# A first work list in another order, with idle matmuls, six strided loads a unit, and constants on another queue

## The chip, the cores and the metric

One core of a Trainium2 chip runs the whole program. The metric is the time of one execution in microseconds of the device. Three runs of the kernel before gave 1581.33, 1581.92 and 1584.39 us, median 1581.92.

## The reference

Retention attention without a softmax, and two feed-forward blocks, all in float32:

```
scores = (q @ k.T) / sqrt(64);  ret = scores * gamma_h**(row - col) for row >= col
x = (ret @ v), heads side by side           # 8 batches, 8 heads, 576 rows, 64 wide -> 4608 x 512
x = ((x @ w1) * (x @ w2)) @ w3 @ w_out      # 512 -> 1024 -> 1024 -> 512
h = x @ w_in;  out = (h - tanh(h)) @ w_out2 # 512 -> 2048 -> 512
```

The weights come in as 64-bit floats, and every product keeps float32 accuracy.

## The kernel before

A product of float32 accuracy is made of three matmuls of a rounded type (`mm3`, L121): each operand is split in a high and a low part. A weight tile (128 x 512) is converted from 64 bit by a `Conv` in steps: `load` (SP's queue), `a` (ScalarE), `b1` to `b4` (VectorE), `c` (ScalarE, the high part), `d1` (the value less its high part, L183) and `d2` (plus the rest, L186). 16 of them, `J[0]` to `J[15]`, make w1 and w2.

Attention runs over 40 chunks, five a batch, of 128 rows (the last of a batch 64). For the first ten the rows are loaded as they lie (256 KB each for q, k and v), scaled, turned on TensorE (`TQ`, `TK`, tiles psq and psk), copied by ScalarE (`CQ`, `CK`), multiplied to scores and to an update of the running state (`SC`, tile psx), masked and summed by VectorE (`PT`, `ST`), and multiplied with v and state (`VA`, tile pso). Then the result is split into its parts x (`RE`, `AD`, `HI`, `LO`). The later 30 chunks are loaded in strided blocks instead, 32 DMAs for half a batch (`load_qk`, L326), which are held in a list `pend` and issued a few at a time by `trickle(n)` (L341) on SP's queue; VectorE then turns them in 32 x 32 blocks (`stage_0`, tiles kT and qT).

The first feed-forward products are 96 units (t, m): 12 tiles of 384 rows by 8 column blocks. A unit is two halves of 12 matmuls (`half_s`, tile psab, four banks), of which ScalarE copies the first (`pf_copy`, L475) and VectorE multiplies the second on (`pf_mult`, L479); the product is stored in DRAM.

Three things set the order. Up to the end of unit 16 it is the list `plan` (L683): a string of tokens, carried out one after the other, where each appends its instructions to its engines' queues. `H0.1.0` is the first half of unit (0, 1), `F`, `G` and `P` its copy, product and store, `Z0` to `Z15` issue four strided loads each, `K`, `X`, `Y`, `V` prepare chunk 10. Behind the list a loop (L760) runs the other 80 units: each starts with up to two steps of a side job (conversions of the other weights, and their product), then the store of an earlier unit, then `trickle(TRK)`, then its two halves, then the attention stages due by a table that places a new chunk every 2.26 units. `need` (L346) issues at once whatever of a tile is still held when a stage wants it. After the units come the two products of the rest, from DRAM.

Each engine carries out its own queue in order; a DMA issued by SP or ScalarE stands in that engine's queue.

Of the kernel before, what the change touches and what calls it, by code (L numbers as in the profile page):

```python
# [8 lines left out]
F32 = mybir.dt.float32  # L9
# [11 lines left out]
P1 = 0.68482121  # L21
# [7 lines left out]
def retention_glu_tanh_kernel(  # L29
# [16 lines left out]
    PE, ACT, DVE, POOL, SP = nc.tensor, nc.scalar, nc.vector, nc.gpsimd, nc.sync  # L46

    B, H, S, D = q.shape
    NT, DM = out.shape
    P = 128  # L50
# [18 lines left out]
    psm = ctx.enter_context(tc.tile_pool(name="psm", bufs=4, space=PSUM))  # L69
# [8 lines left out]
        return slots.tile([P, 2048], F32R, tag=f"s{i}", name=name)  # L78

    cst = cpool.tile([P, 2 * P + 4], F32, name="cst")  # L80
    SP.dma_start(out=cst, in_=consts)
    ident = cst[:, 0:P]
    mask = cst[:, P:2 * P]
    b_p1 = cst[:, 2 * P:2 * P + 1]
# [1 line left out]
    b_mk = cst[:, 2 * P + 2:2 * P + 3]  # L86
    NB32 = S // W
    dec = cpool.tile([P, 2 * H * NA + NP * NB32], F32, name="dec")
    SP.dma_start(out=dec, in_=decay)
    dec_q = dec[:, 0:H * NA].rearrange("p (c h) -> p c h", h=H)  # L90
    dec_v = dec[:, H * NA:2 * H * NA].rearrange("p (c h) -> p c h", h=H)
    dec_b = dec[:, 2 * H * NA:].rearrange("p (g j) -> p g j", g=NP)
# [21 lines left out]
    def tick():  # L114
        for e in held:
            e[0] -= 1
        for _, eng, o, i_ in [e for e in held if e[0] <= 0]:
            eng.dma_start(out=o, in_=i_)
        held[:] = [e for e in held if e[0] > 0]
# [221 lines left out]
    def trickle(n):  # L341
        for _ in range(min(n, len(pend))):
            _, o, i_ = pend.pop(0)
            SP.dma_start(out=o, in_=i_)  # L344
# [152 lines left out]
    def w12_target(m, i):  # L497
        def f(j):
            if i == 0:
                ws[m] = slot(m, f"w12_{m}")  # L500
            j.high = ws[m][:, i * 1024:i * 1024 + 512]
            j.low = ws[m][:, i * 1024 + 512:i * 1024 + 1024]
        return f

    def rows(w):

        return tuple(w[o:o + DM // 2].rearrange("(k p) c -> p k c", p=D) for o in (0, DM // 2))

    J = [
        Conv(rows((w1, w2)[i][:, m * P:m * P + P]), target=w12_target(m, i), pool="head")  # L510
        for m in range(FF) for i in range(2)
    ]
# [115 lines left out]
    ACT.activation(warm, warm, AF.Copy)  # L628
    px = {}
    pu = {}  # L630

    def natural(i, k):
        attn_load(i, "qkv"[k])
# [29 lines left out]
    def four(z):  # L663
# [2 lines left out]
            load_qk(2, 1)  # L666
        trickle(4)

    act = {
        "Lq": lambda i: natural(i, 0), "Lk": lambda i: natural(i, 1), "Lv": lambda i: natural(i, 2),  # L670
        "SQ": lambda i: scale(POOL if i else DVE, A[i][0], dec_q, i),
# [4 lines left out]
        "RE": rest, "AD": add_rest, "HI": x_high, "LO": low_part,  # L676
        "LJ": lambda j: J[j].load(), "a": lambda j: J[j].a(), "c": lambda j: J[j].c(),
        "b1_": lambda j: J[j].b1(), "b2_": lambda j: J[j].b2(), "b3_": lambda j: J[j].b3(), "b4_": lambda j: J[j].b4(),
        "d1_": lambda j: J[j].d1(POOL), "d2_": lambda j: J[j].d2(),
        "H": part_ab, "F": first, "G": second, "P": stored,  # L680
        "Z": four, "K": load_kv, "X": stage_q, "Y": stage_0, "V": stage_v,
    }
    plan = """  # L683
    Lq0 Lk0 Lv0 Lq1 Lk1 Lv1 SQ0 LJ0 TQ0 Lq2 Lk2 TK0 CQ0 Lv2 SV0 CK0 Lq3 Lk3 SC0 SQ1 Lv3 LJ1 PT0 TQ1 ST0 TK1 CQ1
    LJ2 SV1 CK1 VA0 Lq4 SC1 RE0.1 Lk4 HI0.0 AD0.1 HI0.1 Lv4 LO0.0 PT1 a0 LJ3 LO0.1 ST1 SQ2 Lq5 Lk5 b1_0 VA1 b2_0
    Lv5 TQ2 RE1.0 b3_0 RE1.1 AD1.0 c0 TK2 SV2 AD1.1 b4_0 HI1.0 HI1.1 d1_0 LJ4 LO1.0 CK2 LO1.1 CQ2 SQ3 d2_0 TK3
    SC2 CK3 SV3 TQ3 PT2 CQ3 ST2 SC3 a1 b1_1 VA2 PT3 b2_1 RE2.0 RE2.1 AD2.0 c1 AD2.1 ST3 HI2.0 SQ4 HI2.1 LO2.0 a2
    VA3 b3_1 SV4 LO2.1 RE3.0 TK4 b4_1 RE3.1 H0.0.0 CK4 d1_1 LJ5 AD3.1 AD3.0 HI3.1 b1_2 HI3.0 b2_2 Lq6 Lk6 LO3.0
    c2 TQ4 d2_1 Lv6 F0.0 SQ5 LO3.1 Lq7 CQ4 H0.0.1 b3_2 a3 Lk7 b1_3 d1_2 Lv7 b4_2 Lq8 b2_3 SC4 SV5 G0.0 Lk8 TQ5
    c3 d2_2 P0.0 TK5 CQ5 PT4 H0.1.0 CK5 b3_3 a4 b1_4 d1_3 b4_3 VA4 F0.1 b2_4 Lv8 SC5 RE4.0 d2_3 c4 LJ6 AD4.0 a5  # L690
    H0.1.1 b3_4 PT5 d1_4 HI4.0 LJ7 LO4.0 ST5 SQ6 TK6 G0.1 VA5 CK6 P0.1 b4_4 SV6 LJ8 b1_5 TQ6 HI5.0 d2_4 RE5.1
    CQ6 SQ7 LO5.0 H0.2.0 AD5.1 b2_5 HI5.1 LO5.1 c5 b3_5 SC6 F0.2 SV7 b4_5 LJ9 TQ7 PT6 d1_5 TK7 CQ7 ST6 Lq9 CK7
    SQ8 Lk9 TK8 d2_5 Lv9 VA6 CK8 H0.2.1 RE6.0 RE6.1 AD6.0 SV8 AD6.1 HI6.0 HI6.1 LO6.0 LO6.1 SC7 G0.2 P0.2 a6
    b1_6 H1.2.0 PT7 b2_6 ST7 c6 H1.0.0 F1.2 b3_6 a7 b1_7 d1_6 b4_6 H1.2.1 LJ10 b2_7 F1.0 d2_6 c7 b3_7 a8 b1_8
    d1_7 H1.1.0 G1.2 P1.2 b4_7 LJ11 b2_8 H1.0.1 d2_7 c8 b3_8 a9 SQ9 b1_9 b4_8 d1_8 VA7 LJ12 G1.0 b2_9 F1.1
    H1.1.1 SV9 RE7.1 P1.0 d2_8 RE7.0 c9 AD7.0 AD7.1 HI7.0 b3_9 HI7.1 TQ8 G1.1 d1_9 a10 H0.3.0 P1.1 LO7.0 b4_9
    CQ8 LJ13 LO7.1 d2_9 SC8 F0.3 b1_10 b2_10 H1.3.0 a11 PT8 c10 b3_10 ST8 d1_10 H0.3.1 b4_10 LJ14 b1_11 d2_10
    F1.3 VA8 b2_11 a12 G0.3 c11 H1.3.1 P0.3 b3_11 RE8.1 RE8.0 b1_12 d1_11 AD8.0 AD8.1 HI8.0 b4_11 HI8.1 H0.4.0
    LJ15 LO8.0 G1.3 LO8.1 P1.3 d2_11 Z0 H1.4.0 F0.4 b2_12 a13 b1_13 c12 b3_12 Z1 b2_13 d1_12 H0.4.1 F1.4 b4_12
    c13 b3_13 d2_12 d1_13 Z2 H1.4.1 a14 G0.4 b4_13 b1_14 P0.4 d2_13 TK9 Z3 TQ9 a15 G1.4 H0.5.0 b2_14 CK9 CQ9  # L700
    b1_15 P1.4 c14 b3_14 Z4 b2_15 d1_14 SC9 F0.5 b4_14 c15 H1.5.0 PT9 Z5 d2_14 b3_15 VA9 F1.5 b4_15 d1_15 Z6
    H0.5.1 RE9.0 AD9.0 d2_15 HI9.0 LO9.0 Z7 H1.5.1 G0.5 P0.5 H0.6.0 G1.5 K10 P1.5 Z8 H1.6.0 F0.6 X10 X11 Y10 Z9
    H0.6.1 F1.6 Z10 V10 H1.6.1 G0.6 P0.6 Z11 H0.7.0 G1.6 P1.6 H1.7.0 F0.7 Z12 H0.7.1 F1.7 Z13 H1.7.1 Z14 G0.7
    P0.7 G1.7 Z15 P1.7
    """
    for tok in plan.split():
        op = max((o for o in act if tok.startswith(o)), key=len)
# [30 lines left out]
    stages.append((p + 3, cluster, (len(chunks) - 1,)))  # L738
    stages.sort(key=lambda e: e[0])

    TRK = 8
    NO = 84
    side_n = {}
    sn = 0
# [15 lines left out]
    for n, (t, m) in list(enumerate(units))[N0:]:  # L760
# [18 lines left out]
        tick()  # L779
        trickle(TRK)  # L780
        pss = []
# [48 lines left out]
    for n, (t, f) in enumerate(py):  # L830
        p_load(n + 3)
        p_split(n + 2)
        if f == 0:
            pool, tag = (psa, "a") if t % 2 == 0 else (psm, "m")
# [196 lines left out]
```

## Time and profile before

| | |
|---|---|
| median of the runs | 1581.92 us |
| profiled execution | 1582.95 us |
| its span, first to last instruction | 1581.2 us |
| TensorE busy | 1547.8 us (98%), 11312 matmuls |
| VectorE busy | 1075.4 us (68%) |
| ScalarE busy | 773.0 us (49%) |
| POOL busy | 111.3 us (7%) |

The profile is one execution. A busy TensorE is not one at its peak: matmuls overlap, and the clock that was granted to it changes, so the start of one matmul after the other tells more than the length of one. "Idle before" an instruction is the time its engine stood, with what ended the wait behind it.

### The profile page before, as it was taken

The page shows a single profiled execution, that of the slowest core. Times are in us where ns is not written, and L with a number is a line of the kernel's source. Part 1 is how long each engine was busy: PE and PEld are TensorE (multiplying, and loading weights), DVE is VectorE, ACT ScalarE, POOL GpSimd, SP SyncE. Part 2 cuts the span into 40 slices and gives each one's busy share as a digit, 9 for nine tenths or more (in the row PEclk, how much of TensorE's full clock was granted, in tenths as well). Part 3 has the DMA queues.
Part 4 walks back from the last instruction along what each step waited for, and adds up shares of the span by engine and source line. Part 5 has one row for each costly group of instructions (what it writes and reads, how often), then busy time and mean ns, then how long its engine had stood idle before and what let it go on. Part 6 is the DMA issues. An engine that isn't in the chain of part 4 may idle for free.

```text
span 1581.2 us, 28518 instructions
## 1 busy us (share of the span) xinstructions
PE 1547.8 (98%) x11312; PEld 1346.0 (85%) x11312; DVE 1075.4 (68%) x1792; ACT 773.0 (49%) x1408; POOL 111.3 (7%) x102
## 2 busy tenths in 40 slices
PE   6999999999999999999999999999999999999999
PEld 5899889999999998888888888888888888888887
DVE  4884766557543567676477777767777777778676
ACT  3431222222221233444376666676676766767665
POOL 3531211111111000000000000000000000000000
PEclk7999999999999999999999999999999999999999
DMA  9856776575756386776460101010010101010000
GB/s 192 175 124 141 172 175 148 140 175 119 158 163 162 115 263 231 249 242 221 167 246 1 47 7 41 14 40 14 0 54 1 47 7 48 7 40 8 27 1 27
DMA packets 265926, 166.45 MB, mean 105 GB/s; under 512 B 206656, under 2 KB 235840, under 8 KB 264384
## 3 DMA queue, kind: packets, MB, share of 16 engines
q1 hardware_dynamic: 264352, 155.06, 36.6%
q10 hardware_dynamic: 1440, 9.57, 1.6%
q8 instruction: 89, 1.46, 0.4%
q14 instruction: 45, 0.37, 0.1%
HBM read 114.24 MB, written 50.33 MB: 104 GB/s over the span
## 4 chain that ended last, share of the span: by engine, by line
PE 85%; DMA 4%; DVE 4%; SPq 3%; issue 2%; ACT 1%; POOL 0%; DVEq 0%; ACTq 0%
PE psh L126 8%; PE psh L124 8%; PE psout L125 8%; PE psout L126 8%; PE psh L125 8%; PE psout L124 8%; PE psab L124 5%; PE psab L125 5%; PE psab L126 5%; PE psy L126 4%; PE psy L124 4%; PE psy L125 4%; SPq L344 2%; PE pso L416 2%; DMA raw<-in_moe_w_out_dram 1%
## 5 line engine op out<-in xcount | busy, mean ns | idle before, releaser
L124 PE MATMUL psab<-x,w 128*128 128x384 f32 x768 | 263.3, 343 | 7.3 <-ACT pf L475 7.2
L125 PE MATMUL psab<-x,w 128*128 128x384 f32 x768 | 259.6, 338 | 2.3 <-DVE w L186 2.3
L126 PE MATMUL psab<-x,w 128*128 128x384 f32 x768 | 259.1, 337 | 0.0
L124 PE MATMUL psh<-yhl,w2i 128*128 128x512 f32 x576 | 225.5, 392 | 0.0
L126 PE MATMUL psh<-yhl,w2i 128*128 128x512 f32 x576 | 225.3, 391 | 0.0
L125 PE MATMUL psout<-w2o,g 128*128 128x512 f32 x576 | 224.5, 390 | 0.0
L126 PE MATMUL psout<-w2o,g 128*128 128x512 f32 x576 | 224.3, 389 | 0.0
L124 PE MATMUL psout<-w2o,g 128*128 128x512 f32 x576 | 224.2, 389 | 0.0
L125 PE MATMUL psh<-yhl,w2i 128*128 128x512 f32 x576 | 224.0, 389 | 0.0
L920 ACT ACTIVATE g<-w 128x512 fp32r<-128x512 f32 x144 | 90.4, 628 | 168.1 <-DVE w L915 168.1
L908 DVE TENSOR_TENSOR w<-u,psh 128x512 f32<-128x512 f32 x144 | 97.8, 679 | 105.8 <-ACT th L902 105.8
L124 PEld LDWEIGHTS psab<-x,w 128*128 128x128 f32 x768 | 145.9, 190 | 11.0 <-ACT pf L475 8.4
L125 PEld LDWEIGHTS psab<-x,w 128*128 128x128 f32 x768 | 146.0, 190 | 3.4 <-DVE w L186 3.1
L126 PEld LDWEIGHTS psab<-x,w 128*128 128x128 f32 x768 | 146.0, 190 | 0.0
L921 DVE TENSOR_TENSOR g<-w,g 128x512 fp32r<-128x512 f32 x144 | 99.5, 691 | 50.4 <-ACT g L920 50.4
L433 ACT ACTIVATE rest<-pso 128x128 f32<-128x128 f32 x64 | 15.1, 275 | 232.6 <-PE pso L416 232.6
L126 PEld LDWEIGHTS psh<-yhl,w2i 128*128 128x128 f32 x576 | 108.1, 188 | 24.1
L125 PEld LDWEIGHTS psh<-yhl,w2i 128*128 128x128 f32 x576 | 108.2, 188 | 23.6
L124 PEld LDWEIGHTS psout<-w2o,g 128*128 128x128 f32 x576 | 108.1, 188 | 22.9
L125 PEld LDWEIGHTS psout<-w2o,g 128*128 128x128 f32 x576 | 108.1, 188 | 22.6
L126 PEld LDWEIGHTS psout<-w2o,g 128*128 128x128 f32 x576 | 108.1, 188 | 22.6
L124 PEld LDWEIGHTS psh<-yhl,w2i 128*128 128x128 f32 x576 | 108.1, 188 | 22.6
(91 smaller groups left out, 2666.4 us busy)
## 6 DMA issues: line engine op xcount, KB each, us to landing
pdr<-pf SPq DMA_DIRECT2D x96, 192.0 KB, 3.9
pin<-pdr SPq DMA_DIRECT2D x36, 512.0 KB, 4.5
raw<-in_moe_w_out_dram SPq DMA_DIRECT2D x24, 512.0 KB, 4.4
ydr<-ys ACTq DMA_DIRECT2D x9, 1024.0 KB, 4.3
out_dram<-os SPq DMA_DIRECT2D x35, 256.0 KB, 2.2
kn<-in_k_dram SPq DMA_DIRECT2D x32, 256.0 KB, 4.2
vn<-in_v_dram SPq DMA_DIRECT2D x32, 256.0 KB, 4.5
raw<-in_moe_w_dram SPq DMA_DIRECT2D x32, 256.0 KB, 5.7
```

The costliest lines, as they stand in the source:

```text
L124: PE.matmul(ps, lh, rh, start=first, stop=False)
L125: PE.matmul(ps, ll, rh, start=False, stop=False)
L126: PE.matmul(ps, lh, rl, start=False, stop=last)
L344: SP.dma_start(out=o, in_=i_)
L416: PE.matmul(po[y][D * hf:D * hf + D, o * D:o * D + D], lhs, rhs, start=not any(x[:2] == (y, hf) for x in mm[:k]), stop=not any(x[:2] == (y ...
L433: ACT.activation(w, A[i][1 - s][:, KD * D:KD * D + NP // 2 * D].rearrange("p (k q) -> p k q", q=D), AF.Copy)
L908: DVE.tensor_tensor(w, u, h, op=ALU.mult)
L920: ACT.activation(g[:, 0, :], w, AF.Copy)
L921: DVE.tensor_tensor(g[:, 1, :], w, g[:, 0, :].bitcast(F32), op=ALU.subtract)
```

## The change

Four edits. The list is another one: the same tokens in another order, and new tokens `D`, each of which puts so many matmuls of the 128 x 128 identity by itself into TensorE's queue (45 in all); their result is read by nobody. `d1` of the 16 conversions in the list moves from POOL to VectorE. The two constant loads are issued by ScalarE and no longer by SP. `TRK`, the strided loads that each unit behind the list issues, is 6 and no longer 8.

```diff
-    SP.dma_start(out=cst, in_=consts)
+    ACT.dma_start(out=cst, in_=consts)
...
-    SP.dma_start(out=dec, in_=decay)
+    ACT.dma_start(out=dec, in_=decay)
...
+    wps = []
...
+    def warm_up(k):
+        if not wps:
+            wps.append(psm.tile([P, 512], F32, tag="m", name="pswarm"))
+        for _ in range(k):
+            PE.matmul(wps[0][:, :P], ident, ident, start=True, stop=True)
...
-        "d1_": lambda j: J[j].d1(POOL), "d2_": lambda j: J[j].d2(),
+        "d1_": lambda j: J[j].d1(DVE), "d2_": lambda j: J[j].d2(),
...
-        "Z": four, "K": load_kv, "X": stage_q, "Y": stage_0, "V": stage_v,
+        "Z": four, "K": load_kv, "D": warm_up, "X": stage_q, "Y": stage_0, "V": stage_v,
...
-    Lq0 Lk0 Lv0 Lq1 Lk1 Lv1 SQ0 LJ0 TQ0 Lq2 Lk2 TK0 CQ0 Lv2 SV0 CK0 Lq3 Lk3 SC0 SQ1 Lv3 LJ1 PT0 TQ1 ST0 TK1 CQ1
+    Lq0 Lk0 Lv0 LJ0 Lq1 SQ0 Lk1 Lv1 D8 TQ0 Lq2 TK0 CQ0 Lk2 CK0 Lv2 SV0 LJ1 D5 SC0 Lq3 Lk3 PT0 a0 Lv3 b1_0 ST0
...
-    TRK = 8
+    TRK = 6
```

TensorE, from its first matmul on, before: psq and psk are the turned q and k of a chunk, psx its scores and updates, pso its outputs.

```order
L262 MATMUL psq<-cst,qn 128x128 x4
L262 MATMUL psk<-cst,kn 128x128 x4
L297 MATMUL psx<-qT,kT 64x64 x16
L278 MATMUL psx<-vn,kn 64x64 x16
L262 MATMUL psq<-cst,qn 128x128 x4
L262 MATMUL psk<-cst,kn 128x128 x4
L416 MATMUL pso<-pt,vn 64x64 x16
L416 MATMUL pso<-qT,state_127 64x64 x8
```

The same place now, pswarm being the tile of the idle matmuls:

```order
L674 MATMUL pswarm<-cst 128x128 x8
L262 MATMUL psq<-cst,qn 128x128 x4
L262 MATMUL psk<-cst,kn 128x128 x4
L674 MATMUL pswarm<-cst 128x128 x5
L297 MATMUL psx<-qT,kT 64x64 x16
L278 MATMUL psx<-vn,kn 64x64 x16
L674 MATMUL pswarm<-cst 128x128 x7
L416 MATMUL pso<-pt,vn 64x64 x16
L416 MATMUL pso<-qT,state_127 64x64 x8
L262 MATMUL psq<-cst,qn 128x128 x4
L262 MATMUL psk<-cst,kn 128x128 x4
```

Idle matmuls stand ahead of the first transposes, of the scores and of the outputs, and the outputs of chunk 0 go ahead of the transposes of chunk 1.

VectorE in the first conversion, before, from the masks of chunk 0 on (pt masked scores, ct and cf the conversion's tiles, x the parts of the attention's result):

```order
L307 TENSOR_TENSOR pt<-psx,mask_129 128x4x64 x2
L287 COPY state_127<-psx 128x256
L289 TENSOR_TENSOR state_128<-psx,state_127 128x256
L440 TENSOR_TENSOR pso<-pso,rest 128x2x64
L447 TENSOR_TENSOR x<-pso,x 128x4x64
```

And now:

```order
L307 TENSOR_TENSOR pt<-psx,mask_129 128x4x64 x2
L153 TENSOR_SCALAR ct<-raw 128x512
L287 COPY state_127<-psx 128x256
L289 TENSOR_TENSOR state_128<-psx,state_127 128x256
L157 SCALAR_TENSOR_TENSOR cf<-cf,ct 128x512
L162 TENSOR_SCALAR ct<-cf 128x512
L447 TENSOR_TENSOR x<-pso,x 128x4x64
L440 TENSOR_TENSOR pso<-pso,rest 128x2x64
L165 SCALAR_TENSOR_TENSOR ct<-raw,ct 128x512
L447 TENSOR_TENSOR x<-pso,x 128x4x64
L183 TENSOR_TENSOR cf<-cf,w_0_298 128x512
```

The conversion begins between the first masks and the first states, and its d1 (L183) is an instruction of this queue; before, POOL had the 16 of them between its scalings.

SP behind the list, before (raw are weight tiles of the side job, kn and vn of a later chunk, qb_1925 and kb_1926 the strided blocks of batch 3's first half, pdr the stores):

```order
L145 DMA raw<-in_moe_w_out_dram 128x512 x2
L360 DMA kn<-in_k_dram 128x8x64
L360 DMA vn<-in_v_dram 128x8x64
L344 DMA qb_1925<-in_q_dram 32x8x32 x8
L118 DMA pdr_69<-pf 128x384
L344 DMA qb_1925<-in_q_dram 32x8x32 x8
L360 DMA kn<-in_k_dram 128x8x64
L360 DMA vn<-in_v_dram 128x8x64
L145 DMA raw<-in_moe_w_out_dram 128x512
L118 DMA pdr_69<-pf 128x384
L344 DMA kb_1926<-in_k_dram 32x8x32 x8
```

And now, the same blocks as qb_1971 and kb_1972:

```order
L145 DMA raw<-in_moe_w_out_dram 128x512 x2
L360 DMA kn<-in_k_dram 128x8x64
L360 DMA vn<-in_v_dram 128x8x64
L344 DMA qb_1971<-in_q_dram 32x8x32 x6
L118 DMA pdr_69<-pf 128x384
L344 DMA qb_1971<-in_q_dram 32x8x32 x6
L360 DMA kn<-in_k_dram 128x8x64
L360 DMA vn<-in_v_dram 128x8x64
L145 DMA raw<-in_moe_w_out_dram 128x512
L118 DMA pdr_69<-pf 128x384
L344 DMA qb_1971<-in_q_dram 32x8x32 x4
L344 DMA kb_1972<-in_k_dram 32x8x32 x2
```

A weight load of the side job has fewer strided issues ahead of it, and the keys of the half batch go out later.

## Rows read from the trace of the kernel before

**Rows 1.** Windows by stage: length, busy PE PEld DVE ACT POOL, clock, DMA, GB/s.

```profile
0.00:37.00 37.00, 22.90 (x532) 19.74 (x532) 16.90 (x37) 12.18 (x28) 14.64 (x19) 0.79 1.07 190
37.00:81.10 44.10, 41.45 (x596) 37.82 (x596) 38.14 (x70) 19.66 (x44) 22.24 (x16) 0.95 0.80 171
81.10:129.30 48.20, 47.39 (x427) 45.66 (x426) 32.22 (x62) 16.10 (x34) 15.43 (x11) 1.00 0.59 133
129.30:215.00 85.70, 76.74 (x1026) 73.14 (x1026) 59.31 (x117) 21.19 (x51) 13.80 (x12) 0.94 0.72 161
215.00:594.00 379.00, 376.06 (x4417) 358.78 (x4416) 211.53 (x435) 86.45 (x207) 45.17 (x45) 1.00 0.62 161
594.00:1581.20 987.20, 983.29 (x4322) 810.85 (x4320) 717.32 (x1074) 617.38 (x1047) 0.00 (x0) 1.00 0.21 72
```

**Rows 2.** Windows of core 0 with half the granted clock, same columns.

```profile
28.20:38.30 10.10, 6.91 (x162) 6.19 (x155) 6.78 (x15) 3.45 (x11) 4.54 (x4) 0.50 1.15 194
...
154.50:157.70 3.20, 3.20 (x12) 3.20 (x11) 1.07 (x4) 0.66 (x2) 0.00 (x0) 0.50 0.95 189
202.30:208.90 6.60, 4.89 (x40) 4.46 (x44) 2.15 (x4) 1.55 (x3) 0.97 (x1) 0.50 0.97 221
```

**Rows 3.** Chain of waits, 0 to 70 us: start us, us, what.

```profile
5.97 1.11 PE psq L262 x4
...
59.17 0.62 PE psx L297 x32
59.80 0.47 PE psx L278 x32
60.26 0.58 PE psq L262 x4
...
62.11 1.09 PE pso L416 x64
...
63.58 0.17 PE psab L125
```

**Rows 4.** Tile psab, 37 to 129.3 us: count, ns min/median/max, first, last start.

```profile
L124 PE MATMUL psab<-x,w x128: 334/334/687, 37.0 to 128.8; 128*128 128x384 f32 x128
```

**Rows 5.** Timeline of SP, first issues: start us, us, what.

```profile
0.74 0.39 SPq L81 DMA_DIRECT2D cst<-in_consts_dram  x1
...
1.65 0.43 SPq L250 DMA_DIRECT2D qn<-in_q_dram  x1
```

**Rows 6.** Timeline of VectorE, 0 to 40 us: start us, us, what, [idle before].

```profile
22.74 1.52 DVE L186 TENSOR_TENSOR w<-cf,ct 128x512 fp32r<-128x512 f32 x1 [0.50 <-POOL cf L183]
...
38.88 0.68 DVE L186 TENSOR_TENSOR w<-cf,ct 128x512 fp32r<-128x512 f32 x1
```

**Rows 7.** VectorE by line, 0 to 129.3 us: count, busy us, mean ns, idle.

```profile
L447 DVE TENSOR_TENSOR x<-pso,x 128x256 fp32r<-128x256 f32 x18 | 7.3, 413 | 0.3 <-ACT x L443 0.3
```

**Rows 8.** POOL by line, 0 to 129.3 us, same columns.

```profile
L183 POOL TENSOR_TENSOR cf<-cf,w 128x512 f32<-128x512 f32 x16 | 25.0, 1565 | 43.1 <-DVE ct L162 24.4 <-ACT w L180 5.3 <-ACT pf L475 4.0
```

**Rows 9.** Timeline of POOL, 20 to 24 us.

```profile
22.67 1.04 POOL L256 TENSOR_TENSOR qn<-qn,dec 128x512 f32<-128x512 f32 x1
```

**Rows 10.** Timeline of SP's queue, strided loads and a weight load.

```profile
106.20 7.87 SPq L344 DMA_DIRECT2D kb<-in_k_dram  x16
...
193.03 4.94 SPq L344 DMA_DIRECT2D kb<-in_k_dram  x8
198.08 0.40 SPq L145 DMA_DIRECT2D raw<-in_moe_w_out_dram  x1
...
199.00 4.22 SPq L344 DMA_DIRECT2D kb<-in_k_dram  x8
```

**Rows 11.** Timeline of ScalarE, 200 to 204 us.

```profile
202.40 0.66 ACT L149 ACTIVATE cf<-raw 128x512 f32<-128x512 f32 x1 [6.07 <-DMA raw<-in_moe_w_out_dram]
```

**Rows 12.** Waits of TensorE, 129.3 to 215 us: us in total, times, longest.

```profile
PE psab L124 <- ACT pf L475: 6.5, 2, 3.9
```

**Rows 13.** Timeline of VectorE, 212 to 217 us.

```profile
214.92 0.70 DVE L387 STREAM_TRANSPOSE kT<-kb 128x512 f32<-128x512 f32 x1
```

More of the change, by code (lines that the diff above doesn't have):

```diff
@@ L685, in retention_glu_tanh_kernel @@
[L685 to L704, printed above, removed]
+    Lq0 Lk0 Lv0 LJ0 Lq1 SQ0 Lk1 Lv1 D8 TQ0 Lq2 TK0 CQ0 Lk2 CK0 Lv2 SV0 LJ1 D5 SC0 Lq3 Lk3 PT0 a0 Lv3 b1_0 ST0
@@ new lines, in retention_glu_tanh_kernel @@
+    Lq4 SQ1 Lk4 D7 VA0 b2_0 Lv4 TQ1 HI0.0 b3_0 RE0.1 LJ2 TK1 LO0.0 c0 SV1 AD0.1 CQ1 LJ3 HI0.1 b4_0 CK1 LO0.1 SQ2
+    LJ4 D6 SC1 d1_0 Lq5 TK2 PT1 SV2 Lk5 TQ2 CK2 ST1 CQ2 d2_0 D2 SC2 VA1 a1 b1_1 PT2 Lv5 RE1.0 b2_1 RE1.1 AD1.0
+    SQ3 c1 AD1.1 ST2 HI1.1 HI1.0 D8 TQ3 b3_1 LO1.0 SV3 TK3 CQ3 LO1.1 VA2 CK3 b4_1 LJ5 d1_1 SC3 RE2.0 RE2.1 AD2.0
+    SQ4 AD2.1 HI2.0 Lq6 PT3 HI2.1 Lk6 SV4 LO2.0 Lv6 ST3 a2 LO2.1 D9 VA3 d2_1 b1_2 H0.0.0 RE3.1 b2_2 RE3.0 a3
+    AD3.1 AD3.0 HI3.1 b3_2 HI3.0 b1_3 TQ4 c2 LO3.0 H0.0.1 F0.0 b4_2 CQ4 LJ6 LO3.1 d1_2 b2_3 Lq7 TK4 CK4 Lk7 SQ5
@@ new lines, in retention_glu_tanh_kernel @@
+    G0.0 TK5 c3 b3_3 P0.0 SC4 Lv7 CK5 d2_2 TQ5 PT4 SV5 a4 H0.1.0 CQ5 b1_4 d1_3 b4_3 VA4 F0.1 LJ7 b2_4 SC5 RE4.0
+    d2_3 c4 AD4.0 SQ6 a5 H0.1.1 b3_4 PT5 HI4.0 LO4.0 d1_4 TQ6 SV6 G0.1 TK6 CQ6 P0.1 ST5 CK6 b4_4 VA5 LJ8 b1_5
+    SC6 d2_4 RE5.1 HI5.0 AD5.1 a6 SQ7 LO5.0 H0.2.0 HI5.1 PT6 LO5.1 b2_5 TQ7 F0.2 ST6 c5 TK7 b3_5 CQ7 SV7 VA6
+    b1_6 CK7 b4_5 RE6.1 SC7 RE6.0 LJ9 d1_5 AD6.0 d2_5 HI6.0 Lq8 LO6.0 a7 H0.2.1 Lk8 AD6.1 Lv8 b2_6 HI6.1 LO6.1
+    c6 b3_6 H1.1.0 G0.2 P0.2 d1_6 b4_6 LJ10 PT7 H1.0.0 F1.1 d2_6 ST7 a8 H1.2.0 F1.0 SQ8 b1_7 b1_8 b2_7 b2_8 c7
@@ new lines, in retention_glu_tanh_kernel @@
+    H1.1.1 b3_7 SV8 c8 b3_8 F1.2 d1_7 VA7 G1.1 P1.1 b4_7 H1.0.1 RE7.1 RE7.0 LJ11 AD7.1 AD7.0 HI7.1 d2_7 HI7.0
+    LO7.0 a9 TK8 G1.0 TQ8 P1.0 LO7.1 CK8 b4_8 H1.2.1 CQ8 LJ12 d1_8 b1_9 d2_8 Lq9 SC8 Lk9 a10 G1.2 b2_9 P1.2
+    H0.3.0 Lv9 PT8 c9 Z0 b3_9 ST8 H1.3.0 F0.3 d1_9 Z1 b4_9 SQ9 b1_10 H0.3.1 F1.3 LJ13 d2_9 b2_10 a11 Z2 H1.3.1
+    SV9 G0.3 c10 b3_10 b1_11 b4_10 P0.3 H0.4.0 Z3 G1.3 d1_10 b2_11 H1.4.0 P1.3 d2_10 F0.4 LJ14 c11 b3_11 a12
+    b1_12 Z4 d1_11 H0.4.1 b4_11 b2_12 F1.4 LJ15 d2_11 c12 H1.4.1 G0.4 a13 Z5 b3_12 b1_13 d1_12 VA8 G1.4 P0.4
@@ L705, in retention_glu_tanh_kernel @@
+    b4_12 P1.4 H0.5.0 RE8.0 Z6 RE8.1 AD8.0 AD8.1 HI8.0 d2_12 HI8.1 LO8.0 a14 H1.5.0 b2_13 Z7 F0.5 LO8.1 c13
+    b3_13 b1_14 H0.5.1 b4_13 K10 d1_13 Z8 b2_14 H1.5.1 d2_13 c14 G0.5 a15 b3_14 P0.5 F1.5 b1_15 Z9 H0.6.0 d1_14
+    G1.5 b4_14 P1.5 b2_15 Z10 H1.6.0 F0.6 d2_14 c15 b3_15 X10 Z11 TQ9 d1_15 TK9 CQ9 H0.6.1 CK9 b4_15 X11 Y10 Z12
+    V10 SC9 G0.6 H1.6.1 PT9 P0.6 Z13 F1.6 d2_15 VA9 G1.6 Z14 H0.7.0 RE9.0 AD9.0 HI9.0 LO9.0 P1.6 H1.7.0 F0.7 Z15
+    H0.7.1 F1.7 H1.7.1 G0.7 P0.7 G1.7 P1.7
     """
```

## The prediction

> **What bounds the kernel now.** I read the stages first [rows 1]: six stretches of the span, with each engine's busy time, the granted clock and the transfer rate. The reader is to see that TensorE sits idle 14.1 us of the first 37.0, 2.7 of the next 44.1, 0.8 of the next 48.2, 9.0 of the 85.7 after that, 2.9 of the 379 up to 594 us and 3.9 of the last 987. So all that can be won lies before 215 us, and what is won there is kept, because nothing later waits for anything but TensorE. The same rows show two other limits: in the first 37 us the transfers are at 1.07 of the engines' time and 190 GB/s, and from 37 to 81 us VectorE is busy 38.1 of 44.1 us.
>
> The second view is the clock [rows 2]. From 28 to 38 us, in a stretch at 154 us and in one at 202 us the granted clock is 0.50, that is 1.2 GHz, each time behind a wait of TensorE. The price is seen in the chain of waits [rows 3]: four 128-column transposes take 1.11 us at the start and 0.58 us later.
>
> The third is the 16 units of the first list [rows 4]: three lines of 128 matmuls of psab each, from 37.0 to 129 us. At 0.17 us each [rows 3] the 384 are 65.3 us. A chunk of attention at full clock is two transposes of 0.58, scores 0.62, updates 0.47 and outputs 1.09, 3.34 us [rows 3]. Four chunks (13.4 us) stand before the first psab, some five (16.7) behind. So 82.0 of the 92 us are work, and 10 are lost.
>
> **The change part by part.**
>
> *Constants on ScalarE's queue.* SP issues two loads before q of chunk 0, which goes out at 1.65 us instead of 0.74 [rows 5]: 0.9 us for the first transfers, between 0 and 0.9. The transfer engines are full [rows 1], so bytes are not moved faster. The Trainium skill, "DMA: Bandwidth & Descriptors", section "Issuing engines are not separate DMA queues", speaks against more than that: a second issuing engine saves only the time of the issue, and all run on the same 16 engines. The trace's share of 1.07 agrees; by the rule the part is 0.9, no more.
>
> *45 idle matmuls.* Each multiplies a 128 by 128 constant by itself. None is in the trace of before. The nearest row is the transpose of that shape, 0.145 us at full clock and 0.28 at half [rows 3]; the scores show that a plain float32 matmul is two records (16 instructions, x32), so I take two of these, 0.29 and 0.56 as upper bounds, 45 for 13 or 25 us; the lower bound is nothing where they end before what TensorE waits for. They stand where it idles 14.1 us. The first eight can start once the constants land, near 3 us, and at half clock take up to 4.5, so the first transposes start between 5 and 7.5 us, at 5.97 before [rows 3]. What they can give is the clock: 22.9 us of busy time up to 37.0 hold only 13.4 us of work at full speed.
>
> *The order before the first psab.* The weights of conversion 0 are now loaded ahead of chunk 1, and conversion 1 ahead of chunk 3. Before VA3 must land four chunks of three 256 KB tiles and two weight tiles of 512 KB: 4.2 MB, at 190 GB/s 22.1 us, from 1.7 us on: 24. Behind the last stand one scaling on POOL (1.04 [rows 9]), scores and updates (1.1), two states, outputs (1.1) and the hops, some 5 us: 29. By TensorE's own work: 3.0 + 13.4 + 13 = 29.4, plus some 3 for the first stretch at half clock. I take 31 for the first psab, bounds 28 and 46 (all at half clock: 3.0 + 22.9 + 20 or more). That is -6, range -9 to +9.
>
> *d1 to VectorE.* On POOL the 16 of them take 1.57 us on average [rows 8]. The addition d2, of the same shape and also with both inputs in SBUF, takes VectorE 0.68 us alone [rows 6], so VectorE gets 16 x 0.68 = 11 us more. Against that stands what POOL's instructions cost VectorE: the same d2 takes 1.52 us beside a POOL instruction [rows 6, 9], while subtractions that read PSUM take 0.41 on average [rows 7]. VectorE's list work nearly equals TensorE's 82 us behind the first psab, so both ends count: of the 10 us lost at most 5 go by this edit (the others are the half clock at 55 us and the change between shapes), or VectorE is full and half of its 11 us, +5, is added. I take -3, nearer to the row of 1.52 us than to nothing. The Trainium skill, "SBUF — State Buffer", section "Who interferes with whom", says that a VectorE instruction with two SBUF inputs and a GpSimd one that reads SBUF lock each other out whole, and one with a PSUM input does not. The 1.52, 0.68 and 0.41 us agree; by the rule each d1 on POOL can hold VectorE 1.04 us, 16.6 in all, against 11.0, which would make this part -5.6. That POOL's scalings stay, with the same lock, speaks against more.
>
> *The 64 loads Z and TRK.* In the list before, the 64 strided q and k issues come at the end, 16 in 7.87 us [rows 10], 0.49 each, 31 us of SP without a pause. They now begin about three units earlier, between the last weight loads. In the units behind, eight a unit cost 4.94 us [rows 10]; with a store, two key loads every 2.26 units and a weight load SP needs some 6.2 us a unit, where TensorE needs 4.1 + 3.34 / 2.26 = 5.6. So it falls behind: the weight load at 198.08 waits behind eight of them, ScalarE waits 6.07 us for it and the copy of psab stands behind that [rows 11], TensorE's largest wait there [rows 12]. With six, SP needs 5.0. To win are the 9.0 us of idle time and half of 8.1 us at half clock [rows 1, 2], 13. I take -5, not 13, since the same 32 loads a group must still pass; bounds -13 and +4.
>
> The sum: -6 - 3 - 5 = -14 against the profiled execution's own 1582.95 (1581.2 of span and 1.75 around it): 1569. The median of the runs, 1581.92, is 1.0 lower, which I leave in the range.
>
> **The rivals.**
>
> *Only the head gains.* SP's lag behind 129 us comes from loads that wait for earlier loads and for buffers that the conversions hold, not from the number a unit. For: each issue there lasts 0.62 us, not 0.49 [rows 10], as if it waited for earlier loads to land. Against: SP has no pause longer than 0.2 us from 193 to 203 us [rows 10]. Then -6 - 3 and 0: 1574.
>
> *Keys come too late (slower).* With six a unit, 32 loads need 5.3 units instead of 4. By the code the last keys of batch 3's second half are now issued in the unit whose transposes read them, of the later batches one unit ahead. Before, they were out at 203.2 [rows 10] and read at 214.92 [rows 13]: 11.7 us, less a landing of some 2.5; two units (11 us) later nothing is left. VectorE stands for the landing, with the products of psab behind it, and TensorE's four banks fill. Five groups of 3 us, the middle's gain lost: 1582.95 - 9 + 15 = 1589. It decides once SP is over a unit (5.6 us) late there.
>
> *The idle matmuls outlast the waits.* At half clock they are 25 us, in order before real work. The clock then rises late, the first psab stays near 37, and only 3 of VectorE's and none of the middle: 1580.
>
> *VectorE becomes the bound.* The 11 us fall whole between 37 and 110 us, POOL's scalings still hold it: +5 in the list, -6 in the head, 0 behind: 1582.
>
> **How the numbers follow.** My forecast (1563 to 1575) 0.55; only the head 0.19; everything won, under 1563, 0.07; idle matmuls too long 0.06; VectorE bound 0.04; keys late 0.09. The range of 1559 to 1581 holds all but the slow cases and the far end of the best. A difference of 0.2%, 3.2 us, is about what a measurement here tells from none: faster, below 1578.8, is the first three and a little, 0.82; the same 0.08; slower 0.10.
>
> **What would show it.** First psab at 31 (28 to 34) and end of the list near 120; TensorE's granted clock 1.0 in most of 8 to 38 us; no L183 row on POOL, and d2 near 0.69; in the 86 us behind the list under 5 us of waits of psab for the copy of psab. Wrong is the forecast if the first psab is past 36, if the transposes of keys wait for their load by more than 2 us at several places, or if the list still takes 92 us from its first psab.

## The result, and the profile after

The changed kernel takes 1563.32 us, median of four runs (1561.24 to 1568.32); the kernel before took 1581.62 in four runs beside them (1578.90 to 1584.39). The ratio is 0.9889, 95% interval 0.9859 to 0.9918. The profiled execution took 1564.07 us, its span is 1562.3, 18.9 less than before.

The stages of the changed kernel, cut at the same places of the work as [rows 1], in the same columns (first psab, units 6, 16 and 30, last psab):

```profile
0.00:34.00 34.00, 25.09 (x619) 23.51 (x619) 19.84 (x42) 11.95 (x26) 11.26 (x16) 1.00 1.03 195
34.00:76.90 42.90, 41.49 (x668) 38.53 (x664) 37.29 (x79) 21.42 (x48) 10.28 (x8) 0.96 0.89 186
76.90:122.70 45.80, 45.80 (x368) 44.49 (x361) 33.20 (x64) 14.08 (x30) 7.03 (x6) 1.00 0.68 142
122.70:197.40 74.70, 72.70 (x1025) 69.43 (x1025) 58.38 (x116) 21.14 (x51) 11.37 (x11) 1.00 0.77 178
197.40:575.10 377.70, 375.47 (x4418) 358.94 (x4417) 212.01 (x435) 86.27 (x207) 44.52 (x45) 1.00 0.64 162
575.10:1562.30 987.20, 983.30 (x4322) 811.62 (x4320) 717.50 (x1074) 617.62 (x1047) 0.00 (x0) 1.00 0.21 72
```

Stage by stage against [rows 1]: 3.0 us to the first psab, 1.2 and 2.4 in the two halves of the list, 11.0 from unit 16 to unit 30, 1.3 behind that, nothing in the last stage. The largest part lies behind the list, where of the four edits only `TRK` acts directly; the earlier strided loads act there by what the list leaves to SP.

The column has a granted clock of 1.00, 2.4 GHz, for the first 34 us, but its start needs care. The profile's records of the clock begin at 7.3 us, with a rise to 1.00 (at 14.5 in the kernel before), and the column takes a time without a record as 1.00. The first eight idle matmuls, nearly all ahead of 7.3 us, take 0.44 us each and later ones 0.26, so TensorE starts at about half speed here too. Behind 7.3 us one stretch at half clock, 1.2 GHz, is left [rows 2], just behind the first psab:

```profile
34.60:38.00 3.40, 3.40 (x14) 2.96 (x13) 3.36 (x9) 1.89 (x6) 0.64 (x1) 0.50 0.91 162
```

What TensorE waits for from 122.7 to 197.4 us (us in total, times, longest); the first line answers to [rows 12], where it was 6.5:

```profile
PE psab L124 <- ACT pf L475: 0.5, 1, 0.5
PE pso L416 <- DVE state L289: 1.3, 1, 1.3
```

SP's queue there [rows 10], start us, us, what: a store has six strided issues behind it, and a weight load goes out before it. ScalarE's longest wait for such a weight load is 2.74 us, where it was 6.07 [rows 11]:

```profile
188.98 0.84 SPq L145 DMA_DIRECT2D raw<-in_moe_w_dram  x1
189.91 0.38 SPq L118 DMA_DIRECT2D pdr<-pf  x1
190.34 3.16 SPq L344 DMA_DIRECT2D kb<-in_k_dram  x6
```

```profile
187.14 0.68 ACT L149 ACTIVATE cf<-raw 128x512 f32<-128x512 f32 x1 [2.74 <-DMA raw<-in_moe_w_out_dram]
```

The first issues of SP and ScalarE and the first scaling on VectorE [rows 5]. q goes out at 0.74 instead of 1.65, but the decay table now lands last, and the scaling waits for it until 5.91 us (5.23 before, when q came last):

```profile
0.74 0.43 SPq L250 DMA_DIRECT2D qn<-in_q_dram  x1
...
0.74 0.45 ACTq L81 DMA_DIRECT2D cst<-in_consts_dram  x1
1.22 0.60 ACTq L89 DMA_DIRECT2D dec<-in_decay_dram  x1
...
5.91 0.69 DVE L256 TENSOR_TENSOR qn<-qn,dec 128x512 f32<-128x512 f32 x1 [5.91 <-DMA dec<-in_decay_dram]
```

VectorE by line to 122.7 us (count, busy us, mean ns, idle); the first line is the moved d1 [rows 8], the second d2 [rows 6], the fourth answers to [rows 7]:

```profile
L183 DVE TENSOR_TENSOR cf<-cf,w 128x512 f32<-128x512 f32 x16 | 13.6, 848 | 0.4 <-ACT w L180 0.4
...
L186 DVE TENSOR_TENSOR w<-cf,ct 128x512 fp32r<-128x512 f32 x16 | 11.0, 686 | 0.0
L479 DVE TENSOR_TENSOR pf<-pf,psab 128x384 f32<-128x384 f32 x15 | 8.3, 553 | 12.4 <-PE psab L126 9.7 <-issue 1.6 <-ACT w L180 1.0
...
L447 DVE TENSOR_TENSOR x<-pso,x 128x256 fp32r<-128x256 f32 x18 | 7.4, 416 | 0.5 <-ACT x L443 0.5
```

POOL has no L183 row left. VectorE stands 9.7 us for TensorE's products, and TensorE waits only 0.2 us for VectorE from the first psab to the end of the list: there VectorE isn't the bound.

### The profile page after: what moved, and what is told of

The parts are those of the page before. It is cut to its first block, busy times and chain, and to the rows that moved or that the text cites. A ratio compares the mean times of both kernels' runs of the same rounds, so it can differ in the third digit from the quotient of the medians.

```text
span 1562.3 us, 28683 instructions
## 1 busy us (share of the span) xinstructions
PE 1543.8 (99%) x11402; PEld 1346.5 (86%) x11402; DVE 1078.2 (69%) x1808; ACT 772.5 (49%) x1408; POOL 84.5 (5%) x86
## 3 DMA queue, kind: packets, MB, share of 16 engines
q1 hardware_dynamic: 264064, 154.85, 37.2%
## 4 chain that ended last, share of the span: by engine, by line
PE 94%; DVE 3%; DMA 2%; issue 1%; ACT 1%; SPq 0%; ACTq 0%; DVEq 0%
PE psh L126 8%; PE psh L124 8%; PE psout L125 8%; PE psh L125 8%; PE psout L126 8%; PE psout L124 8%; PE psab L124 8%; PE psab L126 7%; PE psab L125 7%; PE psy L126 4%; PE psy L124 4%; PE psy L125 4%; PE pso L416 2%; PE psx L297 1%; PE psx L278 1%; PE psw L124 1%
```

## The experiments

All have one core; the ratio is that to the kernel before, with its 95% interval, and "stretch" is the time from the start of unit 16 to that of unit 30 in the profile (85.7 us before, 74.7 in the changed kernel). One profile of such a stretch is good to some 2 us: six profiles of the changed list with six loads a unit have it at 72.8 to 74.9.

**The loads a unit, each way.** The changed kernel with eight, and the kernel before with six.

```diff
-    TRK = 6
+    TRK = 8      # e1_trk8, in the changed kernel
...
-    TRK = 8
+    TRK = 6      # e2_before_trk6, in the kernel before
```

> The changed kernel with eight strided loads a unit again (TRK 8), the rest as changed. Theory A, the number a unit made the gain behind the list: the list ends at 122.7 us as before this edit, the 14 units behind it take 80 to 85 us and not 74.7, whole time 1568 to 1574. Rival B, the new list made it, since SP comes out of it with less left to do: those 14 units take under 77 us and the time is within 3 us of the changed kernel's 1563.

Measured: 1574.50 us, ratio 0.9963 (0.9950 to 0.9976); stretch 81.0. The first theory held, but 5 to 6 us of gain stay with eight, which the next experiments put down to the earlier loads.

> The kernel before with six strided loads a unit, nothing else changed. Theory A: the list ends at 129 us, the 14 units behind it take 76 to 80 us and not 85.6, whole time 1572 to 1577. Rival B: they take 84 us or more, the time stays within 3 us of before. Rival C, keys come too late with six: over 86 us, and transposes of keys wait for their load; slower than before.

Measured: 1571.13 us, 0.9940 (0.9926 to 0.9954); stretch 79.3, the first theory again. The number alone is worth 9 us in the old list and 11 in the new one. The sign of its cause is the wait of psab for the copy of pf, from unit 16 to unit 30: 6.5 in [rows 12], 0.5 in the changed kernel, and here, with eight in the new list and with six in the old one:

```profile
PE psab L124 <- ACT pf L475: 4.4, 2, 3.1
```

```profile
PE psab L124 <- ACT pf L475: 3.5, 1, 3.5
```

Either way more than half of that wait is left.

**No idle matmuls.** The 45 are left out of the changed kernel (the `D` tokens).

```diff
-    Lq0 Lk0 Lv0 LJ0 Lq1 SQ0 Lk1 Lv1 D8 TQ0 Lq2 TK0 CQ0 Lk2 CK0 Lv2 SV0 LJ1 D5 SC0 ...
+    Lq0 Lk0 Lv0 LJ0 Lq1 SQ0 Lk1 Lv1 TQ0 Lq2 TK0 CQ0 Lk2 CK0 Lv2 SV0 LJ1 SC0 ...
```

> The changed kernel without the 45 idle matmuls, the rest as changed. Theory A, they hold the clock up: without them the granted clock is half for 8 us or more up to 40 us, first psab at 36 to 38 us and not 34.0, the time 2 to 4 us above the changed kernel's. Rival B, they only fill waits that are there anyway, or delay real work: first psab at 34 or earlier, the time the same or up to 3 us lower.

Measured: 1561.76 us, 0.9887 (0.9870 to 0.9904), against 0.9889 with them; first psab at 34.1. The rival held: the idle matmuls are worth nothing that can be measured. They do hold the clock up, as the first theory had it: without them the first rise on record is at 20.0 us and not at 7.3, and two more stretches of 3.4 us at half clock follow by 37. But TensorE's time to the first psab comes out the same. Without them it is 20.4 us of busy time and 13.7 of waits:

```profile
0.00:34.10 34.10, 20.36 (x529) 17.95 (x529) 20.22 (x42) 12.21 (x26) 11.59 (x16) 0.94 1.04 190
```

With them it is 12.0 us of the same work, 8.9 of waits and 13.05 of idle matmuls (25.09 busy in 34.0). They save 8.3 us of slow work and 4.8 of waits, and cost 13.05. What they do in detail is seen in TensorE's timelines. With them (start, us, what, [idle before]): the first transposes run at full clock, 0.60 instead of 1.12 us, but start 0.8 us later, behind 16 records of idle matmuls; and the last outputs before the first psab are cut in two by 2.15 us in which TensorE waits for nothing that the profile names.

```profile
4.22 3.49 PE L674 MATMUL pswarm<-cst 128*128 128x128 f32 x16 [4.22 <-DMA cst<-in_consts_dram]
7.55 0.60 PE L262 MATMUL psq<-cst,qn 128*128 128x128 f32 x4
...
28.31 2.28 PE L674 MATMUL pswarm<-cst 128*128 128x128 f32 x18
30.52 0.69 PE L416 MATMUL pso<-pt,vn 64*64 64x64 f32 x32
31.03 0.41 PE L416 MATMUL pso<-qT,state 64*64 64x64 f32 x15
33.59 0.46 PE L416 MATMUL pso<-qT,state 64*64 64x64 f32 x17 [2.15 <-issue]
33.98 0.44 PE L124 MATMUL psab<-x,w 128*128 128x384 f32 x1
```

Without them the work is slower, the wait that the profile doesn't name is 0.51, and the end is the same:

```profile
6.74 1.12 PE L262 MATMUL psq<-cst,qn 128*128 128x128 f32 x4 [6.74 <-DVE qn L256]
...
26.79 1.26 PE L416 MATMUL pso<-pt,vn 64*64 64x64 f32 x28
...
31.78 0.66 PE L416 MATMUL pso<-pt,vn 64*64 64x64 f32 x8 [1.21 <-DVE x L447]
32.95 0.52 PE L416 MATMUL pso<-pt,vn 64*64 64x64 f32 x21 [0.51 <-issue]
...
34.09 0.69 PE L124 MATMUL psab<-x,w 128*128 128x384 f32 x1
```

**The constants back on SP's queue**, with the idle matmuls, and without them.

```diff
-    ACT.dma_start(out=cst, in_=consts)
+    SP.dma_start(out=cst, in_=consts)
...
-    ACT.dma_start(out=dec, in_=decay)
+    SP.dma_start(out=dec, in_=decay)
```

> The changed kernel with the two constant loads on SP's queue again, ahead of q of chunk 0. Theory A, on ScalarE's queue the constants share the transfer engines with q, k and v and land later: here they land near 2.9 us (4.2 in the changed kernel), the first idle matmul starts then, q of chunk 0 is scaled at 5.2 us and not 5.9, first psab up to 1 us earlier, time the same or 1 us lower. Rival B, the 0.9 us of issue count: everything 0.9 us later, first psab near 35.

Measured: 1566.22 us, 0.9906 (0.9887 to 0.9924): not to be told from the changed kernel. The two transfers land in 2.2 and 2.0 us from SP and took 3.4 and 4.6 from ScalarE, so the first idle matmul starts at 2.97 instead of 4.22, and q is scaled at 5.34 instead of 5.91. So much of the first theory held; the first psab is no earlier (36.4), and the time is not lower.

> The changed kernel without idle matmuls and with both constants issued by SP ahead of q of chunk 0, as before the change. Theory A: with no idle matmul waiting for the constants only the first scaling of q on VectorE needs them (the decay table); on SP it lands 0.6 us sooner and q 0.9 us later, so the first transposes and the first psab move by less than 1 us from those without idle matmuls (first psab 34.1) and the time is within 2 us of 1561.8: the queue of the constants is worth nothing. Rival B: the constants on ScalarE's queue cost the head 1 to 2 us because they land behind the big loads: first psab near 32.5 and 1559 to 1560.

Measured: 1562.25 us, 0.9883 (0.9868 to 0.9899), first psab 34.1. The first theory held: what starts earlier on one queue lands later on the other, and the queue is worth nothing.

**d1 on the other engine, each way.**

```diff
-        "d1_": lambda j: J[j].d1(DVE), "d2_": lambda j: J[j].d2(),
+        "d1_": lambda j: J[j].d1(POOL), "d2_": lambda j: J[j].d2(),   # e5_d1_pool, in the changed kernel
...
-        "d1_": lambda j: J[j].d1(POOL), "d2_": lambda j: J[j].d2(),
+        "d1_": lambda j: J[j].d1(DVE), "d2_": lambda j: J[j].d2(),    # e6_before_d1_dve, in the kernel before
```

> The changed kernel with d1 of the 16 conversions on POOL again, order and all else as changed. Theory A, d1 on POOL holds VectorE and makes it late: the list from first psab to its end takes 91 to 94 us and not 88.7, d2 averages over 0.8 us (0.69 in the changed kernel), time 1566 to 1569. Rival B, VectorE has room and the edit is worth nothing by itself: list within 1.5 us, time within 2 us of 1563.

Measured: 1562.79 us, 0.9886 (0.9868 to 0.9904), the same as with d1 on VectorE, as the rival had it. From first psab to the end of the list 89.2 us (88.7 in the changed kernel). POOL does hold VectorE up: VectorE's L165 has two inputs in SBUF and takes 718 ns on average in the changed kernel, and 1118 here, with d1 on POOL. But d2 takes 698 ns here against 686, and not the over 800 that the first theory expected (same columns as above):

```profile
L183 POOL TENSOR_TENSOR cf<-cf,w 128x512 f32<-128x512 f32 x16 | 22.9, 1436 | 36.2 <-DVE ct L162 19.5 <-ACT w L180 14.2 <-ACT cf L149 2.5
```

```profile
L165 DVE SCALAR_TENSOR_TENSOR ct<-raw,ct 128x512 f32<-128x512 uint32 x16 | 17.9, 1118 | 0.0
```

> The kernel before with d1 on VectorE, nothing else changed. Theory A, POOL's lock costs more than the 11 us of work: the list takes 88 to 91 us from its first psab and not 92.3, time 1576 to 1578. Rival B, VectorE is full in this order and the work comes on top: 94 us or more, slower than before by 2 us or more.

Measured: 1578.66 us, 0.9984 (0.9970 to 0.9997), some 2 us and barely clear of none; from first psab to the end of the list 91.0 (92.3 before), which decides nothing, since three other profiles of the old list, with d1 on POOL, have 91.2 to 92.7.

**The strided loads early, in the old list.** The 16 tokens `Z` of the kernel before stand where the changed list has them: the first behind the 13th half of a unit instead of the 17th, the last behind the 30th instead of the 32nd. SP issues the first of their loads at 79.17 us instead of 95.78. All else is as before.

```diff
-    ... a10 H0.3.0 P1.1 LO7.0 b4_9 ... H0.4.0 LJ15 LO8.0 G1.3 LO8.1 P1.3 d2_11 Z0 H1.4.0 ... b3_12 Z1 ...
+    ... a10 H0.3.0 Z0 P1.1 LO7.0 b4_9 ... H1.3.0 Z1 a11 ... H0.3.1 Z2 b4_10 ... H0.4.0 Z3 LJ15 ... H1.4.0 Z4 ...
```

> The kernel before with its tokens Z put as early among the units as in the new list (the first behind 13 halves and not 17), eight a unit behind the list, nothing else changed. Theory A, SP comes out of the list with less left to do: the 14 units behind the list take 80 to 82 us and not 85.6, time 1575 to 1577. Rival B, SP's place behind the list is set by the loads there, not by what the list leaves: 84 us or more, time within 2 us of before, or the list itself is longer because weight loads wait behind the strided ones.

Measured: 1573.05 us, 0.9952 (0.9936 to 0.9969), 7.8 us less than before; stretch 79.9. The first theory held, and the time fell by more than it had.

**Both edits that give SP room, in the old list**: `TRK = 6` and the early `Z`, nothing else.

> The kernel before with two edits together: six strided loads a unit (TRK = 6) and the 64 loads of group 2 begun three units earlier in the list. Theory A: these two make the middle's gain and add up, because both only give SP room: each alone took 5.7 to 6.3 us off the stretch from unit 16 to unit 30 (85.6 us before) and 9 and 7.6 off the whole; together the stretch is 75 us, as in the changed kernel (74.7), and the time is 1564 to 1567, within 4 us of the changed kernel, so that the new order of the first 16 units, d1 on VectorE, the idle matmuls and the constants' queue together are worth 0 to 4 us. Rival B: both edits remove the same lag, so they do not add: the stretch stays near 79 and the time near 1571, and what the changed kernel has beyond that comes from its new order.

Measured: 1564.24 us, 0.9902 (0.9889 to 0.9915), the first theory. Head and list are those of the kernel before (first psab 36.4, end of the list 129.0), and the stretch has no idle time left:

```profile
129.00:201.10 72.10, 71.97 (x1027) 69.48 (x1026) 56.70 (x116) 21.64 (x52) 11.48 (x11) 1.00 0.79 181
201.10:576.80 375.70, 375.16 (x4417) 358.88 (x4416) 211.33 (x435) 86.35 (x207) 45.19 (x45) 1.00 0.64 163
```

From [rows 1] to the first of these lines TensorE's idle time falls from 9.0 to 0.1 us and its busy time from 76.7 to 72.0, the granted clock rising from 0.94 to 1.00. Why the two edits add is seen in SP's lag, the start of its store in a unit less the start of that unit on TensorE:

| | before | `TRK` 6 | early `Z` | both | changed kernel |
|---|---|---|---|---|---|
| unit 19, us | 10.9 | 9.7 | 4.1 | 2.9 | 5.2 |
| unit 28, us | 7.5 | 2.4 | 8.3 | 2.4 | 3.9 |

The early start takes away the lag with which SP comes out of the list, the smaller number the one that it builds up again behind it. Each leaves the other's.

**How few loads a unit.** Without idle matmuls, five and seven in place of six (`TRK = 5`, `TRK = 7`).

> The changed kernel without idle matmuls and with five strided loads a unit. Theory A, fewer a unit let weight loads and stores through earlier: the 14 units behind the list take 71 to 72 us (72.8 with six and no idle matmuls), time 1559 to 1561. Rival C, keys come too late: transposes of keys wait for their load, in the middle or in the units up to 594 us, and the time is 3 us or more above the 1561.8 of six.

Measured: 1578.68 us, 0.9986 (0.9975 to 0.9997): 17 us more than with six. The stage behind unit 30 takes 388.7 instead of 375.6 us. VectorE's waits for the keys and TensorE's for what VectorE makes of them, from 123 us to the last psab:

```profile
DVE kT L387 <- DMA kb<-in_k_dram: 22.9, 6, 6.1
...
DVE kT L387 <- DMA qb<-in_q_dram: 8.1, 1, 8.1
```

```profile
PE psx L297 <- DVE qT L389: 6.1, 3, 3.6
PE pso L416 <- DVE state L289: 4.8, 2, 3.5
PE pso L416 <- DVE state L287: 1.6, 1, 1.6
```

With six, VectorE waits 2.2 us once for such keys, and TensorE never for it (4.6 in two waits with the idle matmuls). Why five are too few follows from the program: a batch has 64 of these loads and five chunks, one every 2.26 units, so 64 in 11.3 units, 5.7 a unit, are used. With five the list `pend` can't keep up, and `need` issues what is missing when it is wanted: at 274.54 us SP issues nine loads of one key tile in a row, and VectorE's transpose of it starts at 280.69, after a wait of 6.11.

> The changed kernel without idle matmuls and with seven strided loads a unit. Theory A: the time as a function of the loads a unit has its best at six: with eight SP is late (11 us more), with five the keys come late (17 more), and seven lies between six and eight: the stretch from unit 16 to unit 30 is 75 to 78 us and the time 1564 to 1569. Rival B: SP's lag only grows once a unit holds more than it can issue in TensorE's 5.6 us; eight pass that and seven do not, so the stretch stays at 73 and the time at 1560 to 1563.

Measured: 1562.74 us, 0.9901 (0.9884 to 0.9918), the runs 1561.0 to 1569.0; stretch 76.7. The profile speaks for the first theory and the median for the second, but the profiled run, of 1567.5, is one of two near 1568, and the other four are at 1561.0 to 1563.2. Six and seven can't be told apart.

**Idle matmuls in half as many instructions.** 24 of 256 columns in place of 45 of 128.

```diff
-        for _ in range(k):
-            PE.matmul(wps[0][:, :P], ident, ident, start=True, stop=True)
+        for _ in range((k + 1) // 2):
+            PE.matmul(wps[0][:, :2 * P], ident, cst[:, :2 * P], start=True, stop=True)
```

> The changed kernel with 24 idle matmuls of 256 columns in place of 45 of 128: about the same columns in about half the instructions. Theory A: the idle matmuls cost what TensorE stands for its next instructions, which are brought in pieces while the transfers are full (waits named issue, 3.6 us in the first 38, against 0.5 without idle matmuls). With 84 fewer records in front of the first psab those waits fall below 2 us, the first psab starts 1 to 3 us earlier than 34.0, at the same granted clock, and the time is 1560 to 1563. Rival B: the waits named issue are tied to a place in TensorE's instructions that every order passes, not to their number: they stay at 3 us or more and the first psab stays at 34 to 36.

Measured: 1564.40 us, 0.9904 (0.9891 to 0.9917), first psab 37.2. The first theory fell, and the rival is nearer: one wait named issue is left, of 2.86 us, and it only came at another place. The idle matmuls behind it ran at half clock, 0.41 us a record, and stood 4.1 us in front of the last outputs:

```profile
28.23 0.33 PE L278 MATMUL psx<-vn,kn 64*64 64x64 f32 x4 [0.39 <-POOL vn L256]
31.43 0.68 PE L278 MATMUL psx<-vn,kn 64*64 64x64 f32 x28 [2.86 <-issue]
32.04 4.11 PE L674 MATMUL pswarm<-cst 128*128 128x256 f32 x10
36.08 0.69 PE L416 MATMUL pso<-pt,vn 64*64 64x64 f32 x32
```

No version beats the changed kernel: the four best (no idle matmuls with the constants on either queue, d1 on POOL, and the changed kernel) have ratios of 0.9883 to 0.9889.

## Why the prediction was right, and where its steps were not

The time of 1563.3 us lies in the range, 5.7 below the forecast, and the sign was right. The sum was -14; 18.9 us came, and they came from other terms than the sum had them: it had -9 from the head and d1, of which the runs leave 0 to 3 that can be shown, and -5 from the middle, which gave more than twice that. That these errors offset each other is luck.

**What bounds the kernel** held: all of the gain but 1.3 us lies before unit 30, and the last stage is 987.2 in every kernel.

**The head** (-6, first psab at 31) gave -3.0 in these two profiles, and that is within the scatter: profiles of the old list have the first psab at 35.5 to 37.0, of the new one at 33.6 to 37.6. The clock did what was predicted, 1.00 from 7.3 to 34.6 us; an idle matmul took 0.44 us at the start (eight in 3.49) and 0.26 at full clock (five in 1.28), under the bounds of 0.56 and 0.29, and the 45 took 13.05 us, where 13 were reckoned. The step that failed is TensorE's own sum, 3.0 + 13.4 + 13 = 29.4. The constants landed at 4.2 and not at 3.0, since their transfers now run beside those of q, k and v; and 3.6 us of waits named issue and 1.2 for copies by ScalarE were not in it; the work itself was 12.0 us and not 13.4. Together that is the 34.0 measured. The sign that was given for the head, 31 (28 to 34), was met at its end in that profile and missed in three of the nine, past 36. The sum also had no line for the kernel without idle matmuls: they stand in front of real work as much as they speed it up, and nothing is left of them.

**The constants** (0 to 0.9) are worth nothing measurable. The rule cited with that step, that a second issuing engine saves the issue alone (the Trainium skill, "DMA: Bandwidth & Descriptors", "Issuing engines are not separate DMA queues"), agrees with this: q went out 0.91 us earlier, and the 3.4 and 4.6 us to landing took it back.

**d1 to VectorE** (-3): from first psab to the end of the list 92.3 us became 88.7, -3.6, but not by this edit: with d1 back on POOL it is 89.2. That POOL holds VectorE up is real: in the old order, up to the end of the list, d1's move took d2 from 907 to 728 ns and L165 from 1112 to 782; in the new order L165 from 1118 to 718, d2 hardly (698 to 686). This is as the section "Who interferes with whom" of the Trainium skill's "SBUF — State Buffer" would have it. What failed is the next step, that VectorE's list work ends with TensorE's: from unit 6 to unit 16 TensorE is busy 45.80 of 45.80 us and VectorE 33.2, so what VectorE wins there is idle time. In the old order, where VectorE waited 3.9 us for POOL's L183 behind the first psab, the edit is worth some 2 us. That the order does the rest of the 3.6 was not tried by itself, but the waits speak for it: in the list TensorE waits 2.3 us for d2 before, 1.7 with d1 on VectorE, and not at all in the new order with d1 on either engine. Over nine profiles of the new list its end lies at 122.7 to 126.7, over five of the old one at 126.5 to 129.3.

**The middle** (-5, bounds -13 and +4) is the mis-sized term. It gave -11.0, and in the old list -13.6, the whole of the bound. The mechanism was as told: SP's lag, the weight loads behind it, the copy of psab behind those; and the bound was priced rightly, 8.8 us of idle time and 4.8 of busy time at a low clock went in the old list. I took 5 since the same 32 loads a group must still pass; but what delayed the weight loads was not the number of loads that pass in all but how many stand ahead of each, and a list that starts them earlier (two units at its first, one at its last) removes a second lag; the step names the earlier start, as three units, and gives it no price. These two edits alone make 15.3 of the 18.3 us between the medians; whether the earlier end of the list adds to them is open: 2 to 3 us by the ratios and the medians, and the intervals overlap.

**The rivals.** "Only the head gains" is nearly the reverse of what happened. "Keys come too late" is a true mechanism with a price of 17 us (15 was worked out), but it begins between five and six loads a unit, where the 5.7 that are used lie; at six it is seen as 4.6 us of VectorE's time that nobody waits for. Its condition was wrong: at five SP is not late (its lag at unit 28 is 3.2 us), the keys are simply issued too few a unit. "The idle matmuls outlast the waits" is half true, 0.8 us before the first transposes. "VectorE becomes the bound" fell: with d1 on top VectorE is busy 70.5 us from first psab to the end of the list, 70.4 before, and it has the wait of 9.7 us above.

## What to carry to other kernels

Where one queue issues both bulk loads that are wanted later and loads that a running chain wants now, read how far it runs behind its consumer at several places: a lag that it comes with and a lag that it builds up are two faults, each with its own edit. The number of bulk issues between two urgent ones has a floor too, at the rate at which the bulk is used (5.7 a unit here), and the first number below it cost as much here as both edits gave. Work put in to hold the clock up costs its own time in the queue and its instructions, so it must be tried without it.

## What the runs showed of the hardware that was not expected

TensorE seems to wait for its own instructions. In the changed kernel the longer waits named issue come at its records 705, 1217 and 1729, in the kernel before at 449, 705 and 961, with wide idle matmuls at 961: always 193 more than a multiple of 256. The page of the changed kernel lists a queue of 16 KB transfers of the kind instruction:

```profile
q8 instruction: 89, 1.46, 0.4%
```

TensorE's queue has 22,927 records in that trace, 89.6 times 256. So one transfer looks like 256 of its instructions; that is read from these counts and times alone. In the changed kernel they end at 21.0, 32.06 and 50.58 us, and TensorE goes on at 22.56, 33.59 and 52.13, each 1.5 to 1.6 later; with wide idle matmuls one ends at 29.86 and TensorE goes on at 31.43, also 1.57. The waits come where small matmuls (0.02 us apart) use up the instructions quickly while the data transfers are at 1.03 of the engines' time; behind the list, with psab matmuls of 0.17 us, there are none. With five loads a unit one of 1.6 us does come at a psab matmul, record 1985, at 60.2 us in the list. That the transfers of the data delay those of the instructions was not tried by itself.
